# A delta-rule attention and cosine-gated FFN kernel: another order of the same 2196 tasks

## The chip, the cores and the metric

One core of a Trainium2 chip. The time is that of the device for one execution, in microseconds (us); the median of three runs stands for a kernel. Engines are called as in the profile: PE (TensorE; PEld its weight loads), DVE (VectorE), ACT (ScalarE), POOL (GpSimd), SP (SyncE, which here only issues transfers).

## The reference

32 heads (4 batches of 8) run a delta rule over 768 steps with a 48 x 48 state; the outputs, laid side by side, go through a gated FFN.

```python
k_n = k / (np.linalg.norm(k, axis=-1, keepdims=True) + 1e-06)
for t in range(S):                       # S = 768
    y[:, :, t] = q[:, :, t] @ state
    v_old = kt @ state
    state = state + beta_t * outer(kt, vt - v_old)
x = y.transpose(0, 2, 1, 3).reshape(3072, 384)
h = x @ w_in                             # 384 x 2048
g = h * np.cos(h)
out = g @ w_out                          # 2048 x 384
```

## The kernel before, in words

Time is cut into 24 chunks ("units", n = 0 to 23) of 32 steps for all 32 heads. Two units make a pair m; a pair gives 256 tokens, which are one FFN pass p = m (0 to 11).

A unit's tasks are: loads of `k`, `q`, `v` (from unit 8 on `blocks`, a load that feeds a transpose on DVE); `turn` (transposes on PE, copied out by ACT); `gram` (products of keys with keys and queries, 64 matmuls); `gram_keys`, `gram_queries` (DVE); the inverse of a unit triangular matrix; `state` (64 matmuls with the running state); `right` (DVE); `solve` (inverse by right side); `solve_out` (DVE); `update` (32 matmuls) and `update_out` (DVE, the new state); `within` (64 matmuls); `within_out` (ACT); `features` (transposes on PE) and `features_out` (ACT), which give x.

The inverse comes in three ways. Units 0 and 1 are inverted by doubling on PE (`double`, six levels of two halves, 32 matmuls a half here, with copies, transposes and adds between). Pair 1 is inverted in halves, all other pairs whole: the Gram matrix goes to DRAM (`gram_put`), comes back in another layout (`gram_get`), POOL runs `inv` (62 small products and subtractions a pair, 30 for pair 1, lines 818 and 825), and the inverse goes out (`put`) and back (`get`). There is one buffer each for the matrix that comes back, for the inverse and for the tile that `get` fills, so pairs go through this loop one after the other.

FFN passes 0 and 1 run plain: `hidden` (24 matmuls, 2.6 to 2.9 us, a block of h), then `turns`, `rest`, `cos`, `gate` on ACT and DVE, and for pass 0 `out` (8 matmuls of 384 columns, line 1223). From pass 2 on `hidden` is a scheme of 20 `layer` products on sums of blocks (`x_sum`, `in_sums`), and from pass 1 on `out` is seven products per pass on sums of blocks (`left`, `right`), with `collect` on DVE. The sums run on DVE or POOL, by choice.

The weights arrive as 64-bit numbers in 28 transfers (`weights`, t = 0 to 11 of 512 KB for w_in, 12 to 27 of 384 KB for w_out), and each is made into 32-bit ones by `split` (ACT), `shift` (DVE) and `add` (POOL). They land in 8 tiles that also hold the gates.

`warm` tasks (56, line 487) are filler: one product on constants, whose result nobody reads; they are left out once the first `out` product has been emitted, and five more run at the very start.

**What sets the order.** Every task has a number, in the order in which it is added: 0 to 4 the first loads, 5 to 7 beta and the half tiles, 8 to 63 the fillers, 64 `clear`, from 65 the units with the FFN behind them, from 2084 the weights (three numbers in four are split, shift and add). `Order.LINE` lists the numbers in the order in which the tasks are emitted; each engine then runs its own tasks in that order. `Order.OTHER` names the tasks that go to their second choice: a sum to the other of DVE and POOL, a transfer to ACT's queue in place of SP's. Transfers of SP and ACT share eight completion semaphores in turn, so the ninth waits until the first has landed. The cost and due figures given to `add` are not used when the kernel is built.

Of the kernel before, what the change touches and what calls it, by code (L numbers as in the profile page):

```python
# [55 lines left out]
class Order:  # L56

    OTHER = {
        ('gram_put', 2), ('q', 3), ('gram_get', 1), ('inv', 1, 0), ('put', 1), ('gram_put',
        4), ('gram_put', 5), ('v', 7), ('v', 8), ('v', 9), ('blocks', 11, 1), ('gram_put',  # L60
        11), ('put', 5), ('v', 13), ('put', 6), ('gram_put', 15), ('gram_get', 7), ('get',
        15), ('v', 16), ('blocks', 16, 0), ('blocks', 16, 1), ('gram_put', 16), ('blocks',
        18, 1), ('k', 19), ('blocks', 19, 0), ('gram_get', 9), ('get', 19), ('gram_put',
        20), ('v', 21), ('gram_put', 21), ('put', 10), ('gram_put', 22), ('v', 23),
        ('gram_put', 23), ('gram_get', 11), ('right', 4, 4), ('left', 1, 1, 0), ('left', 1,
        3, 0), ('left', 1, 3, 1), ('store', 1, 0), ('x_sum', 2, 'd'), ('x_sum', 2, 'n'),
        ('x_sum', 2, 'm'), ('x_sum', 2, 'e'), ('x_sum', 2, 'k'), ('x_sum', 2, 'g'),
        ('x_sum', 2, 'i'), ('x_sum', 2, 'l'), ('x_sum', 2, 'f'), ('x_sum', 2, 'b0'),
        ('left', 2, 4, 1), ('left', 2, 3, 1), ('x_sum', 3, 'd'), ('x_sum', 3, 'n'),
        ('x_sum', 3, 'm'), ('x_sum', 3, 'e'), ('x_sum', 3, 'k'), ('x_sum', 3, 'g'),  # L70
        ('x_sum', 3, 'i'), ('x_sum', 3, 'l'), ('x_sum', 3, 'h'), ('x_sum', 3, 'b0'),
        ('left', 3, 4, 1), ('left', 3, 3, 1), ('x_sum', 4, 'd'), ('x_sum', 4, 'm'),
        ('x_sum', 4, 'g'), ('x_sum', 4, 'i'), ('left', 4, 3, 0), ('left', 4, 3, 1),
        ('store', 4, 0), ('x_sum', 5, 'd'), ('x_sum', 5, 'e'), ('x_sum', 5, 'l'), ('x_sum',
        5, 'h'), ('x_sum', 5, 'b0'), ('left', 5, 2, 0), ('left', 5, 4, 1), ('left', 5, 3,
        0), ('left', 5, 3, 1), ('store', 5, 0), ('x_sum', 6, 'd'), ('x_sum', 6, 'g'),
        ('x_sum', 6, 'l'), ('x_sum', 6, 'f'), ('x_sum', 6, 'b0'), ('left', 6, 1, 0),
        ('left', 6, 4, 0), ('store', 6, 1), ('x_sum', 7, 'd'), ('x_sum', 7, 'm'), ('x_sum',
        7, 'g'), ('x_sum', 7, 'i'), ('x_sum', 7, 'f'), ('x_sum', 7, 'h'), ('x_sum', 7,
        'b0'), ('left', 7, 4, 0), ('left', 7, 4, 1), ('left', 7, 3, 1), ('x_sum', 8, 'd'),  # L80
        ('x_sum', 8, 'm'), ('x_sum', 8, 'e'), ('x_sum', 8, 'k'), ('x_sum', 8, 'g'),
        ('x_sum', 8, 'l'), ('left', 8, 3, 0), ('store', 8, 0), ('store', 8, 1), ('x_sum', 9,
        'd'), ('x_sum', 9, 'm'), ('x_sum', 9, 'e'), ('x_sum', 9, 'k'), ('x_sum', 9, 'i'),
        ('x_sum', 9, 'l'), ('x_sum', 9, 'b0'), ('left', 9, 1, 0), ('left', 9, 2, 0),
        ('left', 9, 1, 1), ('left', 9, 3, 0), ('store', 9, 0), ('x_sum', 10, 'k'), ('x_sum',
        10, 'i'), ('x_sum', 10, 'l'), ('x_sum', 10, 'h'), ('x_sum', 10, 'b0'), ('left', 10,
        1, 0), ('left', 10, 1, 1), ('left', 10, 4, 1), ('left', 10, 3, 0), ('left', 10, 3,
        1), ('store', 10, 0), ('x_sum', 11, 'd'), ('x_sum', 11, 'e'), ('x_sum', 11, 'k'),
        ('x_sum', 11, 'g'), ('x_sum', 11, 'f'), ('left', 11, 1, 0), ('left', 11, 2, 0),
        ('left', 11, 1, 1), ('left', 11, 3, 0), ('left', 11, 3, 1), ('store', 11, 1),  # L90
        ('store_right', 11), ('weights', 5), ('weights', 7), ('weights', 15), ('weights',
        16), ('weights', 18), ('weights', 20), ('weights', 22), ('weights', 23), ('weights',
        25), ('weights', 27)
# [4 lines left out]
0 1 66 2 70 2084 3 71 4 8 9 72 122 67 68 5 2085 123 69 127 73 128 124 65 75 125 80 76 77 2088 178 78  # L98
82 129 2089 74 2092 64 207 79 81 130 10 2096 132 83 134 181 84 6 179 11 2090 136 135 12 133 87 140
2086 2093 86 210 85 2100 13 14 89 208 90 143 15 88 91 16 2104 141 17 142 182 2097 2094 94 244 211  # L100
183 137 95 2091 185 212 139 138 96 18 93 19 131 144 92 2108 186 215 121 145 2098 245 216 111 184 213
2105 147 97 100 101 20 187 188 2112 98 21 148 2087 22 23 2095 102 268 2101 105 24 146 150 2116 99
2109 189 25 190 217 191 2099 149 103 26 2106 126 269 218 219 106 220 27 104 112 151 2110 107 109 153
221 110 247 251 2107 252 108 152 2113 248 223 2120 28 113 154 249 2124 222 299 114 29 2114 155 2102
156 115 30 2115 117 157 2128 116 2132 160 31 180 2103 2117 118 158 119 120 2136 2125 323 159 168 224
2140 250 272 162 2111 273 163 2121 2133 2118 161 253 2137 169 209 792 225 166 226 254 2122 255 256
227 167 164 32 165 33 170 2119 2138 34 171 172 174 2144 2126 173 274 793 2129 2139 2127 2123 246 228
214 300 35 797 2141 275 276 302 2130 2148 2131 277 175 176 303 2145 2134 794 192 177 2149 193 278
798 306 795 2152 304 307 802 2142 2146 279 194 195 799 2150 196 796 2156 36 197 2135 198 2147 803
804 305 37 199 805 807 270 200 2143 2151 2153 800 201 38 2160 2154 806 203 324 202 308 309 2164 229  # L110
801 812 310 2161 2157 2162 204 205 206 230 808 280 2168 327 813 271 2158 328 231 817 2165 814 232
815 809 233 281 354 378 282 283 234 2166 2169 2159 235 2172 236 2167 816 2176 2155 938 818 7 832 39
40 41 356 931 2163 810 42 237 2173 811 2180 43 2177 2174 822 44 238 357 2184 240 239 284 2170 241
285 827 823 819 2185 2178 935 311 820 833 242 243 45 824 286 2186 821 361 301 2179 825 46 2181 47
258 828 360 48 329 826 49 259 330 860 848 2171 861 829 830 865 2182 831 866 862 870 844 863 867 409
332 287 864 333 871 939 868 2175 936 2183 872 934 2188 869 875 834 334 2187 331 880 873 257 874 260
2192 876 50 382 932 849 358 335 336 2189 2190 325 877 362 433 885 2191 381 261 2193 881 262 2194 878
879 882 264 886 933 263 852 883 890 265 337 887 411 288 266 2195 884 891 289 895 267 338 359 290 888
291 845 856 889 835 892 292 896 355 897 937 383 464 339 947 293 294 836 295 296 838 297 51 298 326
846 313 954 52 415 53 363 379 412 853 488 837 953 941 364 839 365 955 956 893 942 340 964 944 960  # L120
965 384 857 894 466 840 54 416 55 341 901 968 366 957 385 948 898 467 841 387 958 961 966 899 842
342 945 962 946 967 969 959 963 900 903 904 970 850 858 972 417 971 973 56 943 979 388 314 906 854
389 974 413 905 981 386 907 982 909 975 843 976 312 980 315 940 902 436 985 437 911 983 316 847 986
984 390 317 318 949 343 319 912 855 977 320 952 908 987 344 345 913 391 914 438 950 988 989 346 915
991 990 917 57 347 392 470 992 1007 993 321 380 910 322 995 919 348 978 58 994 349 996 414 471 951
393 394 350 920 999 491 1000 1015 997 351 1008 352 395 998 368 353 1016 1066 1009 418 419 1001 420
439 1068 921 1010 1073 440 1067 1011 421 396 1002 922 1003 1069 1005 397 916 442 1004 923 918 1006
1012 443 1017 1074 1013 924 1070 1077 1076 851 1018 1071 1072 367 468 925 1081 1014 1078 1082 1079
1019 1080 927 1075 441 519 859 1085 444 1023 1083 928 1086 1084 369 472 1024 1094 1092 410 929 1095
1093 926 370 59 1020 1036 1021 525 371 434 1098 469 1099 1025 445 1087 1022 1026 398 446 372 374 373  # L130
1035 1038 1096 375 1027 1031 376 1028 399 1029 1097 1032 492 1033 1100 1101 377 1102 1041 400 1030
1034 1104 1088 1103 1039 401 1042 465 1044 1105 1089 1106 402 489 1046 1037 403 1124 1108 404 1125
1090 1091 543 1047 473 405 1040 930 474 1109 447 493 1120 1048 406 1110 475 1049 435 1126 407 423
408 526 1121 1179 1122 448 494 1050 1181 1107 449 1127 495 1051 1052 1111 476 497 1054 1114 496 450
1055 451 1128 452 60 1115 1043 424 1129 1182 1183 1056 1112 1057 1118 1058 1180 498 1130 1123 1045
1119 521 1113 1184 422 522 1186 61 1185 1190 1194 574 1059 1060 1116 1191 1131 598 1132 62 1053 1133
# [1738 lines left out]
```

## Time and profile before

| | us |
|---|---|
| median of three runs (641.67 to 646.46) | 642.42 |
| the profiled execution | 642.72 |
| its span, first to last instruction | 640.9 |
| PE busy, fillers included | 616.0 |
| DVE busy | 510.5 |
| POOL busy | 441.5 |
| ACT busy | 296.4 |
| moved by DMA | 50.38 MB, 79 GB/s mean |

The page gives each engine's busy time and 40 slices of 16 us. The mean granted clock of PE is 0.986. Some landmarks of the timeline, in us from the span's start: solve-0 begins at 47.76, hidden-0-0 at 64.12, solve-2 at 85.81, update-3 at 111.49, and the last matmul ends at 637.2.

### The profile page before, as it was taken

The page shows a single profiled execution, that of the slowest core. Times are in us where ns is not written, and L with a number is a line of the kernel's source. Part 1 is how long each engine was busy: PE and PEld are TensorE (multiplying, and loading weights), DVE is VectorE, ACT ScalarE, POOL GpSimd, SP SyncE. Part 2 cuts the span into 40 slices and gives each one's busy share as a digit, 9 for nine tenths or more (in the row PEclk, how much of TensorE's full clock was granted, in tenths as well). Part 3 has the DMA queues.
Part 4 walks back from the last instruction along what each step waited for, and adds up shares of the span by engine and source line. Part 5 has one row for each costly group of instructions (what it writes and reads, how often), then busy time and mean ns, then how long its engine had stood idle before and what let it go on. Part 6 is the DMA issues. An engine that isn't in the chain of part 4 may idle for free.

```text
span 640.9 us, 25243 instructions
## 1 busy us (share of the span) xinstructions
PE 616.0 (96%) x10688; PEld 570.7 (89%) x10688; DVE 510.5 (80%) x1049; ACT 296.4 (46%) x528; POOL 441.5 (69%) x780
## 2 busy tenths in 40 slices
PE   5877999999999999999999999999999999999997
PEld 4655877897799999999999999999999999999997
DVE  5776877998989899887898888888888786656682
ACT  3444655654334453553642544643643553545440
POOL 5435888888778788788689888886883884112231
PEclk9887999999999999999999999999999999999999
DMA  9777556563551454434536245243304202000000
GB/s 189 200 177 180 113 157 145 93 141 54 100 88 20 98 87 70 86 69 73 88 68 104 49 70 99 49 67 67 74 2 78 45 3 41 19 2 26 2 25 26
DMA packets 209369, 50.38 MB, mean 79 GB/s; under 512 B 200920, under 2 KB 204264, under 8 KB 209256
## 3 DMA queue, kind: packets, MB, share of 16 engines
q1 hardware_dynamic: 161896, 35.03, 28.7%
q10 hardware_dynamic: 47072, 13.25, 10.1%
q8 instruction: 84, 1.38, 0.9%
q0 software_dynamic: 288, 0.50, 0.4%
q14 instruction: 29, 0.24, 0.1%
HBM read 38.51 MB, written 10.22 MB: 76 GB/s over the span
## 4 chain that ended last, share of the span: by engine, by line
PE 82%; DMA 7%; DVE 4%; issue 2%; SPq 2%; POOL 1%; ACT 1%; ACTq 0%; DVEq 0%; POOLq 0%
PE p_out L1281 28%; PE p_h L1199 27%; PE p_h L1025 6%; PE p_out L1223 3%; PE p_kq L869 3%; PE p_s L966 3%; PE p_kq L983 3%; DMA kp<-in_k_dram 3%; PE p_u L941 2%; PE p_g L648 2%; PE p_h L1281 2%; PE p_z L1004 1%; DMA g_ffn<-in_moe_w_in_dram 1%; SPq L392 1%; DMA z_dr<-z 1%
## 5 line engine op out<-in xcount | busy, mean ns | idle before, releaser
L818 POOL TENSOR_TENSOR part<-z,gb 128x126 f32<-128x126 f32 (+23 forms) x321 | 146.1, 455 | 41.8 <-DMA gb<-g_dr 12.9
L825 POOL TENSOR_TENSOR z<-z,part 128x126 f32<-128x126 f32 (+23 forms) x321 | 146.9, 458 | 25.1
L1281 PE MATMUL p_out<-w_out,g_ffn 128*128 128x192 f32 x672 | 121.9, 329 | 0.6 <-DVE o L1333 0.6
L1281 PEld LDWEIGHTS p_out<-w_out,g_ffn 128*128 128x128 f32 x672 | 107.7, 190 | 2.0 <-DVE o L1333 0.9
L1078 ACT ACTIVATE turns<-turns,halfpi 128x512 f32<-128x512 f32 x96 | 68.0, 718 | 55.0 <-DVE turns L1069 43.0
L1281 PE MATMUL p_out<-w_sum,g_ffn 128*128 128x192 f32 x496 | 89.7, 329 | 0.2 <-DVE o L1333 0.2
L1199 PE MATMUL p_h<-x_sum,w_in 128*128 128x128 f32 x640 | 84.0, 277 | 0.0
L1062 ACT ACTIVATE turns<-g_ffn,quarter_turn 128x512 int32<-128x512 f32 x70 | 49.8, 719 | 66.7 <-DVE g_ffn L1216 29.5
L1281 PEld LDWEIGHTS p_out<-w_sum,g_ffn 128*128 128x128 f32 x496 | 79.6, 190 | 1.2 <-issue 0.4
L1199 PEld LDWEIGHTS p_h<-x_sum,w_in 128*128 128x128 f32 x640 | 78.8, 192 | 1.1
L1216 DVE TENSOR_TENSOR g_ffn<-g_ffn,p_h 128x512 f32<-128x512 f32 x80 | 54.2, 680 | 17.3 <-PE p_h L1199 16.4
L1069 DVE SCALAR_TENSOR_TENSOR turns<-g_ffn,turns 128x512 f32<-128x512 f32 x70 | 54.3, 783 | 13.0 <-ACT turns L1062 12.9
L996 ACT COPY y<-p_kq 32x384 f32<-32x384 f32 x96 | 45.1, 470 | 36.4 <-PE p_kq L983 30.0
L1081 DVE TENSOR_TENSOR g_ffn<-turns,g_ffn 128x512 f32<-128x512 f32 x70 | 51.9, 751 | 3.8 <-ACT turns L1078 3.7
L567 POOL TENSOR_TENSOR knrm<-ksum,halves 128x16 f32<-128x16 f32 (+1 forms) x14 | 38.4, 2745 | 22.8 <-DVE ksum L555 20.7
L1199 PE MATMUL p_h<-x_sum,in_sum 128*128 128x128 f32 x400 | 52.9, 277 | 0.0
L1199 PEld LDWEIGHTS p_h<-x_sum,in_sum 128*128 128x128 f32 x400 | 49.7, 192 | 0.8
L1333 DVE SCALAR_TENSOR_TENSOR o<-p_out,o 128x192 f32<-128x192 f32 x74 | 25.1, 351 | 29.3 <-PE p_out L1281 28.8
L1025 PE MATMUL p_h<-x_ffn,w_in 128*128 128x128 f32 x384 | 46.1, 277 | 0.0
L1025 PEld LDWEIGHTS p_h<-x_ffn,w_in 128*128 128x128 f32 x384 | 44.2, 192 | 1.4 <-issue 0.2
L1199 PE MATMUL p_h<-x_ffn,w_in 128*128 128x128 f32 x320 | 42.4, 277 | 0.0
L1297 POOL TENSOR_TENSOR g_ffn<-g_ffn,g_ffn 128x512 f32<-128x512 f32 x18 | 25.4, 1417 | 23.2 <-PE p_out L1281 19.4
(156 smaller groups left out, 1080.8 us busy)
## 6 DMA issues: line engine op xcount, KB each, us to landing
g_ffn<-in_moe_w_in_dram SPq DMA_DIRECT2D x10, 512.0 KB
gb<-g_dr SPq DMA_DIRECT2D x14, 256.0 KB
vp<-in_v_dram SPq DMA_DIRECT2D x68, 48.0 KB
g_ffn<-in_moe_w_out_dram SPq DMA_DIRECT2D x8, 384.0 KB
g_ffn<-in_moe_w_out_dram ACTq DMA_DIRECT2D x8, 384.0 KB
kp<-in_k_dram SPq DMA_DIRECT2D x120, 24.0 KB
out_dram<-o SPq DMA_DIRECT2D x14, 192.0 KB
zt<-z_dr SPq DMA_DIRECT2D x72, 32.0 KB
```

Source lines behind the costliest of these rows:

```text
L567: nc.gpsimd.tensor_tensor(out=scales[m][2][:, part], in0=sums[m, part.start][:, 0:n], in1=halves[:, 0:n], op=ALU.pow,)
L818: eng.tensor_tensor(out=part, in0=z[:, 0:rows, j, None].to_broadcast(shape), in1=a[:, j, None, j + 1 :].to_broadcast(shape), op=ALU.mult,)
L825: eng.tensor_tensor(out=behind, in0=behind, in1=part, op=ALU.subtract)
L996: nc.scalar.copy(by_parity(y[quarter(b)]), p_kq[quarter(b ^ 1), :, b % 2])
L1025: nc.tensor.matmul(p_h[:, i], w_in[:, t, (4 * k + i) * 128 : (4 * k + i + 1) * 128], xts[p][:, t, unit * 128 : (unit + 1) * 128], start=(i ...
L1062: nc.scalar.activation(turns[p, f], hidden_of(p, f), AF.Identity, bias=quarter_turn, scale=TURN)
L1069: nc.vector.scalar_tensor_tensor(out=r, in0=hidden_of(p, f), scalar=TURN, in1=t, op0=ALU.mult, op1=ALU.subtract,)
L1078: nc.scalar.activation(r, r, AF.Sin, bias=halfpi, scale=2.0 * math.pi)
L1081: nc.vector.tensor_tensor(out=place(p, f), in0=step_of(rests.pop((p, f)), f), in1=step_of(hidden_of(p, f), f), op=ALU.mult,)
L1199: nc.tensor.matmul(p_h[:, e], in_block(*w)[:, e], x_of(p, b), start=new and e == 0, stop=True, skip_group_check=True,)
L1216: nc.vector.tensor_tensor(out=part_of(p, to), in0=part_of(p, one), in1=part_of(p, two), op=op)
L1281: nc.tensor.matmul(p_o, left(p, part, a)[:, e % 4], right(e, b), start=(e == 0), stop=(e == FT // 2 - 1), skip_group_check=True,)
```

## The change

Two constants of `Order` are replaced; no task, tile, instruction or size is changed. `WARM_FIRST` (5) and `WARMS` (56) stay, and with the new place of the first `out` two fillers less are emitted (29 for 31). The diff, cut to the beginning of both constants:

```diff
     OTHER = {
-        ('gram_put', 2), ('q', 3), ('gram_get', 1), ('inv', 1, 0), ('put', 1), ('gram_put',
-        4), ('gram_put', 5), ('v', 7), ('v', 8), ('v', 9), ('blocks', 11, 1), ('gram_put',
...
+        ('k', 2), ('gram_put', 2), ('q', 3), ('gram_put', 3), ('inv', 1, 1), ('put', 1),
+        ('q', 5), ('gram_put', 6), ('v', 7), ('gram_get', 3), ('gram_put', 8), ('blocks',
...
     LINE = """
-0 1 66 2 70 2084 3 71 4 8 9 72 122 67 68 5 2085 123 69 127 73 128 124 65 75 125 80 76 77 2088 178 78
...
+8 0 1 9 2084 70 178 66 2088 2 3 71 207 122 181 4 67 10 5 11 68 2092 123 72 179 69 73 127 75 12 128
...
```

Read as names, PE's tasks up to update-3 (a number after "warm" counts fillers in a row; `double` has unit, level and half):

```
before
turn-0 warm2 gram-0 turn-1 double-0-0-1 double-0-0-0 gram-1 warm1 double-0-1-0 double-1-0-0
warm2 double-0-1-1 double-1-1-0 warm3 double-0-2-0 warm2 double-0-2-1 double-1-0-1 turn-2 warm2
double-1-1-1 turn-3 double-0-3-0 double-0-3-1 warm1 gram-2 warm1 double-1-2-0 warm2 double-0-4-1
warm2 gram-3 double-0-4-0 warm2 double-1-2-1 double-0-5-0 double-0-5-1 turn-4 warm1 solve-0
double-1-3-0 warm1 update-0 warm1 within-0 double-1-3-1 double-1-4-0 warm1 features-0 state-1
turn-5 double-1-4-1 gram-4 hidden-0-0 double-1-5-1 double-1-5-0 warm2 solve-1 warm1 update-1
within-1 gram-5 warm1 hidden-0-2 features-1 state-2 turn-6 hidden-0-4 solve_half-2 warm1 between-2
warm1 solve-2 hidden-0-6 update-2 warm1 within-2 gram-6 hidden-0-8 features-2 state-3 turn-7
hidden-0-10 solve_half-3 between-3 solve-3 out-0-0-0 hidden-0-12 update-3

after
warm2 turn-0 warm2 gram-0 turn-1 warm2 gram-1 double-0-0-0 double-0-0-1 warm2 double-0-1-1
double-1-0-1 turn-2 double-0-1-0 warm1 double-0-2-1 warm1 turn-3 warm1 double-0-2-0 gram-2
double-1-0-0 warm2 double-0-3-0 warm1 double-1-1-1 warm2 double-1-1-0 warm1 double-0-3-1 gram-3
warm1 double-0-4-1 double-0-4-0 double-1-2-0 double-0-5-0 turn-4 warm1 double-0-5-1 double-1-3-0
warm1 double-1-2-1 solve-0 warm1 update-0 double-1-4-0 within-0 warm2 features-0 state-1 turn-5
double-1-3-1 hidden-0-0 gram-4 double-1-4-1 double-1-5-0 double-1-5-1 warm2 solve-1 hidden-0-2
update-1 within-1 gram-5 warm1 state-2 features-1 warm1 turn-6 hidden-0-4 warm1 solve_half-2
between-2 solve-2 warm1 update-2 within-2 gram-6 out-0-0-0 features-2 state-3 turn-7 hidden-0-6
solve_half-3 hidden-0-8 between-3 hidden-0-10 solve-3 hidden-0-12 update-3
```

Fillers apart, the two hold the same tasks up to update-3. The transfers of the head, a star for those on ACT's queue (a `k`, `q` or `v` is four transfers, 192 KB together; a `gram_put` 128 KB here):

```
before
weights-0 v-0 weights-1 k-2 weights-2 k-3 weights-3 q-2 weights-4 q-3* weights-5* k-4 weights-6 v-1
q-4 weights-7* k-5 weights-8 gram_put-2* q-5 gram_put-3 weights-9 weights-10 gram_get-1* k-6
weights-11 weights-12 v-2 weights-13 k-7 weights-14 v-3 gram_put-4* weights-15* v-4 put-1*

after
weights-0 k-2* weights-1* k-3 weights-2 q-2 weights-3 q-3* weights-4* weights-5 v-0 weights-6 k-4
k-5 weights-7 v-1 gram_put-2* weights-8 q-4 weights-9* weights-10 k-6 gram_put-3* weights-11*
gram_get-1 q-5* weights-12* k-7 v-2 q-6 weights-13* weights-14* v-3 weights-15 weights-16*
gram_put-4 q-7 put-1*
```

On ACT's own line `k-2` now stands ahead of the first `square-0-0`, and `weights-1` ahead of `turn_out-0`. POOL's adds of the weights and `inv-1` are shuffled (`inv-1-0` moves from DVE to POOL, `inv-1-1` the other way), and `beta_home` comes early on DVE. Later in the kernel the same kinds of tasks are permuted: 51 `x_sum` and 32 `left` sums change between DVE and POOL (`left` on POOL: 33 before, 29 after; `x_sum` 46 and 47), two `right` sums and one of `in_sums` likewise, and 74 groups of transfers change queue.

## The prediction

> **What bounds the kernel now.** I read the page's engine totals and slices first, then who TensorE (PE) waited for, the chain of waits, PE's timeline over the first 100 us and the windows table.
>
> ```profile
> span 640.9 us, 25243 instructions
> PE 616.0 (96%) x10688; PEld 570.7 (89%) x10688; DVE 510.5 (80%) x1049; ACT 296.4 (46%) x528; POOL 441.5 (69%) x780
> PE   5877999999999999999999999999999999999997
> DMA  9777556563551454434536245243304202000000
> q8 instruction: 84, 1.38, 0.9%
> ```
>
> PE is full from the fifth slice on; only the head has room. "Busy" includes the filler products of line 487 (72 matmuls, whose rows in the timeline sum to 26 us), all before 92.6 us. Idle (640.9 - 616.0 = 24.9 us) plus filler is 51 us, the most that any order could save. The last line is PE's code: 84 packets for 2 x 10688 instructions, 254 each, so one packet for every 127 matmuls with their weight loads.
>
> ```profile
> PE p_u L935 <- issue: 4.0, 2, 2.7
> PE p_g L648 <- issue: 3.3, 3, 1.7
> PE p_out L487 <- issue: 1.6, 1, 1.6
> ```
>
> These waits end on nothing that the profile names. In PE's timeline they stand in the middle of one product:
>
> ```profile
> 16.47 0.42 PE L648 MATMUL p_g<-kq_t 48*32 48x64 f32 x4 [1.18 <-issue]
> 29.45 0.81 PE L487 MATMUL p_out<-o 128*128 128x256 f32 x3 [1.59 <-issue]
> 35.12 0.83 PE L648 MATMUL p_g<-kq_t 48*32 48x64 f32 x47 [1.66 <-issue]
> 44.73 0.73 PE L710 MATMUL p_h<-in_sum 32*32 32x32 f32 x62 [0.93 <-issue]
> 51.24 0.31 PE L935 MATMUL p_u<-vp,in_sum 32*32 32x48 f32 x10 [2.70 <-issue]
> 87.96 0.28 PE L935 MATMUL p_u<-g_ffn,w_sum 32*32 32x48 f32 x4 [1.28 <-issue]
> ```
>
> Counted from the start they stand at matmul 218, 471, 597, 852, 977 and 1992: whole multiples of some 126.7 apart. They are ends of code packets. The trace's DMA records give each packet's start, and for each I subtract the time at which PE crossed the boundary before: 1.04, 4.63, 3.10, 2.44, 1.17, 3.95, 1.89, 1.67, 1.82, 2.25 us for the ten from 17.51 to 66.80 (mean 2.4), and 0.4 to 1.9 for most later ones. The packet then takes 0.9 to 1.5 us, and PE goes on 1.35 to 1.5 us after it. So a boundary costs nothing if PE needs over about 3.5 us (1.04 + 1.08 + 1.39) to work through a packet, and up to 7 where transfers are outstanding: at 44.73 two weight loads had just been issued (43.93, 44.55) and the packet started 3.95 us later. The six waits sum to 9.3 us.
>
> ```profile
> 48.54 2.70 issue
> 52.80 1.56 PE p_s L966 x32
> 54.36 1.15 PE p_out L487 x2
> 69.38 4.59 DMA z_dr<-z
> 86.68 1.28 issue
> ```
>
> The chain of waits holds only two of them, 2.70 and 1.28. Before 40 us it runs over the loads of k, q and the weights, later over the inverse and its trip through DRAM.
>
> ```profile
> 50.00:60.00 10.00, 8.34 (x240) 6.09 (x243) 7.62 (x20) 2.41 (x6) 4.43 (x4) 0.66 0.68 178
> ```
>
> In this window the granted clock is 0.66, after the 2.70 us wait. update-0, filler and within-0 take 4.2 us there (chain, 52.80 to 56.99); the same three from 91.11 take 2.26. So the slow clock costs 1.9.
>
> The Trainium skill (TensorE: Matmul & The Clock Gate, Part 1) puts a halved clock after an idle window of some 3.4 us; here 2.70 us of idle was followed by it.
>
> **The change, part by part.** All 2196 tasks stay. I lay the new PE order out by matmuls per task (64 for a gram or state, 32 for an update or half a doubling level, 24 for a hidden, 2 for a filler). On the old order this puts matmul 218 at the 61st of gram-1 and 977 in solve-0, as the trace has it.
>
> *Start.* Loads k-2 and weights-1 go to ScalarE's queue, ahead of square-0-0 and turn_out-0. In their lane places the old order's v-0 was issued from 8.01 to 10.74 and weights-1 until 11.24; ScalarE can only go on after that. So square-0-0 moves from 8.43 to about 10.8 and turn_out-0 from 8.84 to 11.3; behind them wait sum-0-0, the roots on POOL and gram-0: the first doubling starts 2.4 us late. Against that q-2 and q-3 have a weight and a load less ahead (704 KB, 3.7 us at the 192 GB/s of the first 50 us). q-4, which turn-4 needs, moves behind weights-7, k-5, gram_put-2 and weights-8 (4928 KB ahead become 6272): 7.0 us. Its last part was issued at 34.66; with 4.5 us to land (the chain's kp loads: 4.0 to 5.8) it is there at 46.2, where turn-4 ran at 45.53. Solve-0 is still behind turn-4, so the early gains end there. Value: 0.
>
> *Solve-0.* Its boundary stays in it (25th of 64 instead of the 55th), and the one before is in turn-4. Between them PE has half a turn, two fillers, three half levels (0.45 to 0.65) and 24 matmuls: about 3.4 us. At the mean queue time a packet needs 2.4 + 1.1 + 1.4 = 4.9, leaving a wait of 1.5 for 2.70; at the ends 0.1 and 3.7. But turn-4 comes 0.7 later. Gain 0.3 (-1.0 to 2.6). Half of the slow clock goes with a wait of that size (35.12's 1.66 left 0.83 in its window): 1.0 (0 to 1.9).
>
> *Solve-2.* Its boundary moves from the 61st matmul to its end. A wait there lies beside solve_out (1.02 on DVE), which update-2 needs anyway: gain 1.2 (0 to 1.28).
>
> *Filler.* Six instead of seven after hidden-0-0, where PE has other work: 0.65 (0 to 0.7).
>
> *Blocks without FFN work.* hidden-0-0 moves ahead of gram-4, hidden-0-2 behind solve-1, and hidden-0-6 behind state-3, out-0-0-0 (2.75 us) ahead of it. Between matmuls 1358 and 1485 PE now has two and a half half levels, two fillers and 38 matmuls of solve-1, 2.8 us; before, hidden-0-0 (3 us) lay in it. The packet needed 2.25 + 0.93 + 1.4 = 4.6 there. It stands before solve_out-1, behind which DVE has update_out-1 and a weight's shift. Loss 1.8 at most, none if the copies and adds between the levels fill it: 1.0. Likewise 1612 to 1738 (2.4 us of matmuls, hidden-0-2 gone) and 1992 to 2118 (3.1 us, hidden-0-6 gone), where packets needed 3.6 and 3.8: 0.5 each (0 to 1.9 together), as DVE's update_out (0.94) and solve_out run meanwhile.
>
> *After 115 us.* PE then idles 1.3 us in all. The left sums on POOL fall from 33 to 29 (1.27 us each, 0.69 to 0.74 on DVE): DVE has 4 to 18 us idle in each 50. The inverse loop has little room: put(3) 172.17, put(4) 210.43, put(5) 252.28; z is back about 4 us after the gets' last issue (176.76, 216.69, 259.16), and solve-6, 8 and 10 start at 181.5, 223.43 and 264.58: slack 0.7, 2.7, 1.4. By PE work ahead, solve-6 comes 2.1 later and 8 and 10 come 2.4 earlier. Loss 0.8 (0 to 3).
>
> Sum: 0.3 + 1.0 + 1.2 + 0.65 - 1.0 - 1.0 - 0.8 = 0.35. The profiled execution took 642.72 (span 640.9), 0.3 over the median of 642.42: 642.4, or 642.1 as a median.
>
> **Rivals.**
> *Packets come early (0.20).* If queue times fall to 1.0, the head gives 2.6 + 1.9 + 1.28 + 0.65, and the earlier q-2 and q-3 net 1.3 (3.7 less 2.4): 7.7, or 634.7. For: eight of the first ten packets came within 1.9 us of being needed. Against: the bytes are the same, and weights issued by solve-1 rise from 10880 to 11840 KB with the loads.
>
> *Packets come late (0.16).* The new order has four packets without FFN work from 1358 to 2118, the old one two (which cost 0.49 and 1.28). If they queue like the one at 44.73, each needs 3.95 + 1.05 + 1.35 = 6.4 against some 3.0 of work; three of four so hit cost 3 x 3.4 - 1.8 = 8.4: 650.8. It decides from a queue time of about 3.3. For: the earlier weights just named. Against: old queue times from 64 to 94 us were 0.7 to 2.3.
>
> *The inverse loop binds (0.12).* A head that gains, with POOL's loop not earlier, gives it back at solve-8 and solve-10: 2.4 + 1.0 in place of the 0.8 above, 642.1 + 2.6 = 644.7.
>
> *Crossing a packet costs nothing (0.05).* Were the gaps something else that stays, only order noise is left: 642.4.
>
> The Trainium skill (Runtime: NRT & Kernel Launch, Instruction fetch mechanics) says that crossing a 16 KiB block is mostly hidden, and gives PE room for 2048 instructions; by that this last rival would hold. The trace agrees on 16 KB but not on hidden: six gaps, 9.3 us.
>
> **How the numbers follow.** The forecast, losses and gains near balance, has 0.47. A measurement here tells about 1% (6.4 us) from no change. Faster: the first rival and a tail of the forecast, 0.20 + 0.02. Slower: the second, with tails of the third and the forecast, 0.16 + 0.03 + 0.04. Same: 0.55. The range runs between the first two rivals' times, 634.5 to 650.5, which leaves a part of each outside.
>
> **What would show it.** square-0-0 at 10.8 and gram-0 near 12.4; turn-4 at 46 or later; a gap inside solve-0 after its 24th matmul, about 1.5 us; granted clock above 0.66 in 50 to 60; a gap inside solve-1 where there was none; no gap inside solve-2; idle ahead of solve-8 or solve-10. I am wrong if turn-4 runs well before 45 (the loads are faster than by bytes), if update-3 ends over 3 us from 112.3, or if PE idles over 4 us after 120.

## The result, and the profile after

The new order is slower by about 1%: 649.94 us (median of 12 runs, 646.39 to 653.01) against 643.18 (639.08 to 646.46), ratio 1.0105 [1.0082, 1.0128]. That is 6.8 us, inside the forecast's range and on the other side of its forecast of 642.1.

The page of the new order (profiled execution 649.79, span 648.0): engine totals, PE's busy tenths, the granted clock and DMA in 40 slices, and the code packets.

```profile
span 648.0 us, 25196 instructions
PE 618.8 (95%) x10684; PEld 571.4 (88%) x10684; DVE 511.2 (79%) x1051; ACT 295.5 (46%) x528; POOL 433.6 (67%) x778
PE   6688879999999999999999999999999999999997
PEclk8989899999999999999999999999999999999999
q8 instruction: 84, 1.38, 0.9%
```

The span grew by 7.1: PE is busy 2.8 longer with two fillers (four matmuls) less, and idle 4.3 longer. Both are to be explained. Some of PE's waits, in us in total, times and longest:

```profile
PE p_g L648 <- issue: 4.6, 2, 3.4
PE p_out L1281 <- DVE o L1333: 1.6, 2, 1.2
PE p_kq L869 <- issue: 1.6, 1, 1.6
PE p_u L941 <- DMA zt<-z_dr: 1.0, 1, 1.0
PE p_u L935 <- issue: 0.9, 1, 0.9
```

The 2.70 in solve-0 and the 1.28 in solve-2 are gone. New are a code wait of 0.9 in solve-1, one in state-2 (L869) and, far behind the head, waits for DVE (L1333) and for z (L941). ("Code wait" is used for a wait at the end of a code packet.) PE's timeline shows where they stand:

```profile
32.23 0.33 PE L648 MATMUL p_g<-kq_t 48*32 48x64 f32 x11 [3.41 <-issue]
46.18 0.63 PE L615 MATMUL p_t<-consts,qp 128*128 128x128 f32 x4 [1.98 <-DMA kp<-in_k_dram]
67.80 0.52 PE L935 MATMUL p_u<-rhs,w_sum 32*32 32x48 f32 x26 [0.94 <-issue]
77.36 0.81 PE L869 MATMUL p_kq<-st,kq_t 48*64 48x48 f32 x21 [1.61 <-issue]
87.61 0.88 PE L935 MATMUL p_u<-g_ffn,w_sum 32*32 32x48 f32 x64 [0.84 <-DVE g_ffn L919]
93.43 0.54 PE L648 MATMUL p_g<-kq_t 48*32 48x64 f32 x35 [1.24 <-issue]
326.36 0.68 PE L941 MATMUL p_u<-rhs,zt 64*64 64x48 f32 x30 [0.96 <-DMA zt<-z_dr]
400.14 1.57 PE L1281 MATMUL p_out<-w_out,g_ffn 128*128 128x192 f32 x8 [1.23 <-DVE o L1333]
```

67.80, 77.36 and 93.43 are matmuls 1485, 1740 and 2119 from the start: the ends of the three packets that the prediction named as having no FFN work. The 3.41 in gram-2 (32.23) lies ahead of solve-1, to which the new order still comes earlier.

Landmarks tell where the time went. Up to solve-1, up to solve-2 and up to update-3 the two orders have done the same tasks, fillers apart.

| us from the start | before | after | after less before |
|---|---|---|---|
| solve-1 | 69.06 | 66.24 | -2.8 |
| solve-2 | 85.81 | 87.61 | +1.8 |
| update-3 | 111.49 | 114.54 | +3.05 |
| last matmul ends | 637.22 | 644.33 | +7.1 |

So the new order leads by 2.8 at solve-1, loses 4.6 on the 20 us to solve-2, 1.25 more to update-3, and 4.06 in the long rest ("the tail" from here on). Of the 4.6, 4.5 are lost by the start of solve_half-2 (82.64 before, 84.35 after); the way from there to solve-2 takes 3.26 for 3.17. The chain of waits of after, between solve-1 and solve-2, whole lines in order of time, with the places marked where lines are left out:

```profile
66.86 0.94 issue
67.80 0.52 PE p_u L935 x26
68.32 2.88 PE p_h L1025 x24
...
75.31 1.11 SPq L841
...
79.30 1.63 DMA w_sum<-z_dr
80.94 0.34 DVE w_out L529
...
81.74 1.09 DVE w_out L529
82.83 1.29 DVE g_ffn L524
84.12 1.09 DVE w_out L529
...
87.09 0.47 DVE g_ffn L919
87.57 0.04 issue
87.61 0.93 PE p_u L935 x64
```

Behind the code wait in solve-1 the chain runs over the way back of pair 1's inverse (`get` on SP, L841, until 80.94) and then through DVE: three steps of the weights' `shift` (L524, L529) and steps of a norm stand ahead of between_out-2 (L919), for which solve-2 waits. The 1.61 in state-2 is not on this chain, so by the profile its removal alone would not have brought solve-2 forward in this execution; in e6 and e10 below, which have the same order here, the chain does run through state-2's wait (1.08 and 0.52) and then over ACT and the same DVE steps. Before, two fillers stood between solve_half-2 and solve-2, and solve-2's one wait was the 1.28 of code.

### The profile page after: what moved, and what is told of

Its sections match the earlier page's. It is cut to its first block, busy times and chain, and to the rows that moved or that the text cites. A ratio compares the mean times of both kernels' runs of the same rounds, so it can differ in the third digit from the quotient of the medians.

```text
span 648.0 us, 25196 instructions
## 1 busy us (share of the span) xinstructions
PE 618.8 (95%) x10684; PEld 571.4 (88%) x10684; DVE 511.2 (79%) x1051; ACT 295.5 (46%) x528; POOL 433.6 (67%) x778
## 4 chain that ended last, share of the span: by engine, by line
PE 73%; DMA 7%; DVE 6%; POOL 5%; SPq 3%; issue 2%; ACT 2%; ACTq 1%; DVEq 0%; POOLq 0%
PE p_out L1281 24%; PE p_h L1199 23%; PE p_h L1025 6%; PE p_out L1223 4%; PE p_kq L869 3%; PE p_s L966 3%; POOL part L818 2%; DMA kp<-in_k_dram 2%; POOL z L825 2%; PE p_kq L983 2%; PE p_g L648 2%; PE p_u L941 2%; DMA g_ffn<-in_moe_w_in_dram 2%; SPq L392 1%; PE p_z L1004 1%
## 5 line engine op out<-in xcount | busy, mean ns | idle before, releaser
L818 POOL TENSOR_TENSOR part<-z,gb 128x126 f32<-128x126 f32 (+24 forms) x321 | 144.5, 450 | 39.8 <-DMA gb<-g_dr 15.9
L825 POOL TENSOR_TENSOR z<-z,part 128x126 f32<-128x126 f32 (+24 forms) x321 | 143.8, 448 | 25.2
L1281 PE MATMUL p_out<-w_out,g_ffn 128*128 128x192 f32 x672 | 124.0, 330 | 1.9 <-DVE o L1333 1.6
L1281 PE MATMUL p_out<-w_sum,g_ffn 128*128 128x192 f32 x496 | 88.2, 328 | 0.0
L1297 POOL TENSOR_TENSOR g_ffn<-g_ffn,g_ffn 128x512 f32<-128x512 f32 x14 | 18.8, 1346 | 66.7 <-PE p_out L1281 45.4
L1069 DVE SCALAR_TENSOR_TENSOR turns<-g_ffn,turns 128x512 f32<-128x512 f32 x70 | 53.0, 759 | 8.5 <-ACT turns L1062 8.3
L1333 DVE SCALAR_TENSOR_TENSOR o<-p_out,o 128x192 f32<-128x192 f32 x74 | 25.0, 350 | 30.3 <-PE p_out L1281 26.9
L1025 PE MATMUL p_h<-x_ffn,w_in 128*128 128x128 f32 x384 | 45.8, 277 | 0.0
L1211 ACT COPY p_h<-p_h 128x512 f32<-128x512 f32 x40 | 22.9, 573 | 46.0 <-PE p_h L1199 33.1
```

Source lines behind the costliest of these rows:

```text
L818: eng.tensor_tensor(out=part, in0=z[:, 0:rows, j, None].to_broadcast(shape), in1=a[:, j, None, j + 1 :].to_broadcast(shape), op=ALU.mult,)
L825: eng.tensor_tensor(out=behind, in0=behind, in1=part, op=ALU.subtract)
L1025: nc.tensor.matmul(p_h[:, i], w_in[:, t, (4 * k + i) * 128 : (4 * k + i + 1) * 128], xts[p][:, t, unit * 128 : (unit + 1) * 128], start=(i ...
L1069: nc.vector.scalar_tensor_tensor(out=r, in0=hidden_of(p, f), scalar=TURN, in1=t, op0=ALU.mult, op1=ALU.subtract,)
L1281: nc.tensor.matmul(p_o, left(p, part, a)[:, e % 4], right(e, b), start=(e == 0), stop=(e == FT // 2 - 1), skip_group_check=True,)
```

## The experiments

Each kernel ran side by side with the kernel before; ratios are to that. Orders are given as names, PE's tasks unless an engine is named.

**Head or tail.** Three splices of the two orders at a task behind which both have done the same work.

```diff
 e1: before's order through update-3
+    then after's order
 e2: after's order through update-3
+    then before's order
 e3: after's order through hidden-0-0
+    then before's order
```

> Every engine's order and every choice of engine or queue is the old one through update-3 and the new one behind it. My theory: the new kernel is 7.1 us longer in the profile because its head loses 3.0 us by update-3 and its steady part 4.1 us behind it; this kernel then pays only the 4.1: ratio to before about 1.006. Rival A, the whole loss is the head's (the later waits follow from it): 1.000. Rival B, the whole loss is the steady part's: 1.011.

> The other way round: new order through update-3, old behind it. My theory: 3.0 us over before, ratio about 1.005, update-3 begins at 114.5 in the profile and the old steady part adds no wait of its own. Rival A (all in the head): 1.011. Rival B (all behind it): 1.000, which needs update-3 to begin near 111.5.

> New order through hidden-0-0, old behind it. In the profiles the new order begins features-0 1.9 us and hidden-0-0 4.05 us earlier, with the gram-4 and doubling work put off. My theory: that lead of some 2 us is real, and what loses it and 5 us more is the new order from solve-1 to out-0-0-0, whose code packets hold no FFN work; with the old order there the lead stays: 2 us under before, ratio 0.997, and no gap in state-2 or gram-6. Rival: the lead is not worth anything, because the weights or the inverse of pair 1 set solve-2 (82.6 to 85.8 in before) whatever comes first: ratio 1.000 to 1.003, solve-2 at 85.8 or later.

Measured: e1 648.83, 1.0092 [1.006, 1.0124]; e2 651.24, 1.0137 [1.0098, 1.0176]; e3 643.47, 1.0009 [0.9983, 1.0035]. The splices bring waits of their own at the seam, 2.0 us in e1 (hidden-1-0) and 4.0 in e2 (hidden-0-14), so the two shares can't be added; by the medians both halves of the new order lose, against both rivals, which put all in one of them. e3 says more: the new order's lead at hidden-0-0 is worth nothing (0.997 was expected), and by the medians of e2 and e3 the head's loss lies behind that point. But e3's profiled execution, the slowest of its twelve (647.59), lost in the old order as well: 48.3 us from solve-1 to update-3 (before: 42.4), with a code wait of 1.56 in solve-1, whose packet has lost hidden-0-0 here too, and one of 2.38 in gram-5, at matmul 1613, where the packet had queued 4.2 us (before: 0.7).

**The two loads on ACT.** after with k-2 and weights-1 back on SP's queue.

```diff
 OTHER = {
-    ('k', 2), ('weights', 1),
```

> The new kernel with loads k-2 and weights-1 on SP's queue instead of ScalarE's, nothing else changed. All theories: square-0-0 back near 8.4 and gram-0 near 10. My theory: turn-4 still waits for q-4 until about 46, so solve-0 begins within 0.5 us of the new kernel's 50.36 and the time stays within 2 us of the new kernel (ratio to before 1.008 to 1.011). Rival: the 2.7 us late start is carried through: solve-0 near 48, ratio 1.006.

Measured: 648.56, 1.0093 [1.0058, 1.0127]. gram-0 came at 9.9 for 12.7 and solve-0 at 48.7 for 50.4, nearer to the rival's 48; but update-3 came no earlier (115.8 for 114.5), and the tail's 529.8 stayed. The late first doubling is real, and the lead of 1.7 at solve-0 that its removal gives is gone by update-3.

**Covering the empty packets.** e5 puts an FFN group into the second packet without one, e8 also into the third.

```diff
 e5, on after:
 gram-5 warm1
+hidden-0-4
 state-2 features-1 warm1 turn-6
-hidden-0-4
 e8, further:
 solve-2 warm1
+hidden-0-6
 update-2 within-2 gram-6 out-0-0-0 features-2 state-3 turn-7
-hidden-0-6
```

> The new order with one group moved: hidden-0-4 runs directly before state-2 instead of behind turn-6, so the code packet during which the new order has no feed-forward group holds one, and its boundary falls on state-2's 19th matmul instead of its 44th. Theory (the 1.61 us wait inside state-2 and the half clock behind it delay right-2, and with it solve_half-2 and solve-2): the wait goes, solve_half-2 starts near 82.4 instead of 84.35, solve-2 near 85.7 instead of 87.61, ratio to the kernel before 1.007 to 1.008 against 1.0105 for the new order. Rival (the inverse and VectorE set solve-2 in any case): solve-2 stays at 87.6, ratio 1.0105 or above, the group's own time being added ahead of it.

> The new order with two groups moved: hidden-0-4 directly before state-2 as in the run above, and hidden-0-6 directly before update-2, behind solve-2, so that the second packet without feed-forward work holds one too. Theory: besides the 1.61 us in state-2, the 1.24 us wait in gram-6 and the half clock at 94.6 to 98.0 go (out-0-0-0 2.7 us instead of 4.38), update-3 starts 3 to 5 us before 114.54, ratio to the kernel before 1.003 to 1.006, the rest being the tail's. Rival (the waits only move with the packet's end to the next task, and the groups lengthen the way to solve-2 or update-2 by their own time): update-3 at 114 to 116, ratio 1.010 or above.

Measured: e5 651.34, 1.012 [1.0074, 1.0165]; e8 649.58, 1.0101 [1.0071, 1.0131]. Neither can be told from the new order's 1.0105, so neither theory held. The code waits in state-2 and (e8) in gram-6 went, and others took their place. PE's timeline of e8:

```profile
81.04 1.19 PE L1019 MATMUL p_w<-rhs,w_sum 32*32 32x48 f32 x64 [1.23 <-ACT kq_t L745]
82.86 0.88 PE L1019 MATMUL p_v<-g_ffn,in_sum 32*32 32x48 f32 x64 [0.62 <-ACT g_ffn L1031]
86.32 1.50 PE L1055 MATMUL p_u<-g_ffn,w_sum 32*32 32x48 f32 x64 [2.58 <-DVE g_ffn L1039]
```

solve_half-2 (81.04) now waits 1.23, and solve-2 (86.32) 2.58 for DVE's between_out-2. One group of 2.9 us covers either the packet or the way from state-2 to solve-2 over ACT and DVE; in the old order hidden-0-2 lay in the packet, and hidden-0-4 covered the way. DVE in the same execution, with the idle time in brackets:

```profile
80.39 1.17 DVE L649 TENSOR_SCALAR w_out<-w_out 128x384 uint32<-128x384 uint32 x1
81.47 1.37 DVE L644 SCALAR_TENSOR_TENSOR g_ffn<-g_ffn 128x384 uint32<-128x384 uint32 x1
82.77 1.17 DVE L649 TENSOR_SCALAR w_out<-w_out 128x384 uint32<-128x384 uint32 x1
84.06 0.99 DVE L700 TENSOR_TENSOR krec<-knrm 128x16 f32<-128x16 f32 x1
85.72 0.55 DVE L1039 TENSOR_TENSOR g_ffn<-rhs,p_v 128x384 f32<-128x384 f32 x1
```

between_out-2 (85.72) stands behind two shifts and a norm.

**Moving the packets instead of the work.** before, with fillers left out so that each packet ends 12 matmuls later in the work. (Five fillers of two matmuls at the start and one behind turn-0; the expectation names the places wrongly.)

```diff
-    WARM_FIRST, WARMS = 5, 56
+    WARM_FIRST, WARMS = 0, 56
 turn-0
-warm2
+warm1
 gram-0
```

> The kernel before, its order untouched, with 12 filler matmuls fewer on TensorE (5 at the start, 7 behind turn_out-0), so that every code packet's end falls 12 matmuls later in the work: the one inside solve-0 and the one inside solve-2 come to lie outside the solves, the next in the same stretch in the gram of layer 1. Theory (the 2.70 us in solve-0 and the 1.28 us in solve-2 are late code, fixed to the matmul's number): both waits vanish from the solves, the solve's end and update-0 come 1.5 to 2.7 us earlier, the wait reappears outside the solves or not at all, ratio 0.995 (0.992 to 0.999). Rival (the waits belong to the products' data, or the fillers kept the clock up and their lack costs 1 to 2 us): the waits stay at the same matmuls of the solves, ratio 1.000 to 1.003.

Measured: 644.23, 1.0019 [0.9995, 1.0043]. PE's timeline:

```profile
46.37 0.89 PE L1053 MATMUL p_u<-vp,in_sum 32*32 32x48 f32 x63 [0.73 <-ACT kq_t L743]
50.76 0.45 PE L828 MATMUL p_h<-w_sum 32*32 32x32 f32 x31 [3.46 <-issue]
75.76 1.01 PE L766 MATMUL p_g<-kq_t 48*32 48x64 f32 x50 [2.93 <-issue]
```

The wait left solve-0 (46.37, 63 of its 64 matmuls in one piece) and stands behind it at the same matmul number, 977 (50.76). So these waits are code, bound to the count of matmuls and not to the data. The time did not fall: a wait just behind the solve costs as much, and the packet that ends at matmul 1613 cost 2.93 inside gram-5. Before, it ended at gram-5's third matmul, just behind a wait for the new state (0.49), and cost nothing. The place is not the reason, since e3 lost 2.38 at before's place: the packet queued 4.6 us here, 4.2 in e3 and 0.7 before.

**The tail's two waits.**

```diff
 e6, on after:
 SP:
+get-13
 k-20
-get-13
 DVE:
-right-16
 collect(5,5)
+right-16
```

> The new order with two steps put back ahead of what the search placed before them: get-13 ahead of k-20's transfers on SyncE's queue, right-16 behind the last step of collect(5,5) on VectorE. Theory (the tail's loss is new waits on other engines that the search made by moving small steps): TensorE's 0.96 us at solve-13 and 1.23 us at out-5-5-0 go, the time from update-3 to the last matmul falls from 529.8 to about 527.6, ratio to the kernel before 1.007. Rival (the waits move to the next task, the tail is bound elsewhere): the two gaps shrink but the stretch stays at 529 to 530, ratio 1.0105.

Measured: 648.27, 1.0076 [1.005, 1.0103]; update-3 to the last matmul 528.4, between theory and rival. The wait at solve-13 is gone, so it was get-13's place: in after SP issued it at 322.06, behind k-20's eight transfers from 316.87. The other wait moved one product ahead, and ACT's timeline of e6 shows why:

```profile
396.53 0.72 ACT L1198 ACTIVATE turns<-turns,halfpi 128x512 f32<-128x512 f32 x1 [7.95 <-DMA g_dr<-g]
397.16 0.58 ACT L1331 COPY p_h<-p_h 128x512 f32<-128x512 f32 x1
```

ACT did nothing for 7.95 us, because transfers of its own queue (block loads, a Gram store) were waiting in its line; cos(6) and the copy that PE needed came behind them.

**All repairs at once, and the queues by themselves.** e9 is e8 with between_out-2 ahead of shift-16, get-13 as in e6, and five transfers back on SP. e10 is after with all such transfers of the tail on SP; e12 is before with 38 more of them on ACT.

```diff
 e9, on e8:
 OTHER = {
-    ('blocks', 20, 1), ('blocks', 21, 0), ('v', 19), ('gram_put', 18), ('put', 8),
 DVE: right-2 shift-17
+scale-3-0
 shift-15
+between_out-2
 shift-16
-scale-3-0 between_out-2
 e10, on after:
 OTHER = {
-    ('v', 7), ('gram_get', 3), ('k', 12), ('k', 13), ('gram_put', 8), ('blocks', 10, 1),
...
 SP:
+get-13
 k-20
-get-13
 e12, on before:
 OTHER = {
+    blocks and gram_put of the tail
```

> The new order with all repairs that the traces suggest. Head: the two feed-forward groups moved as in the run before (hidden-0-4 ahead of state-2, hidden-0-6 ahead of update-2), and on VectorE between_out-2 ahead of the weights' shift-16, which took it 2.2 us too late there. Tail: get-13 ahead of k-20 on SyncE, and blocks-20-1, blocks-21-0, v-19, gram_put-18 and put-8 back from ScalarE's queue to SyncE's, since ScalarE stood 6.79 us on such transfers with cos(6) behind them. Theory (feed-forward groups cover either a packet or the way over VectorE to solve-2, and the tail waits on a queue that stands in ScalarE's line): solve_half-2 to solve-2 shrinks from 5.3 us to about 3.3, VectorE's 2.58 us wait ahead of solve-2 to under 0.8; the waits at solve-13 and out-5-5-0 go without a new one, update-3 to the last matmul 527.5 instead of 529.8; ratio to the kernel before 1.003 to 1.005. Rival (another chain stands right behind each): solve-2 waits as long on something else, the stretch stays above 528.4, ratio 1.008 or above.

> The new order, its head untouched; behind update-3 the 37 transfers that go to ScalarE's queue (all but the stores of passes 9 to 11) are put on SyncE's, and get-13 stands ahead of k-20. Theory (the tail's waits of 2 us, which came back at another place in each repaired version, come from transfers standing in ScalarE's own line: ScalarE stood 6.79 us ahead of cos(6) and 7.16 us ahead of collect(3,1) on them): no wait above 0.5 us behind update-3, update-3 to the last matmul 526.8 to 527.3 (the 525.7 of the old order and five more changes of kind at 0.2), ratio to the kernel before 1.005 to 1.007. Rival (SyncE's queue becomes the late one, or the waits come from the order of the products themselves): waits of 2 us or more in all stay or grow, stretch at or above 528.4, ratio 1.008 or above.

> The kernel before, its order untouched; behind update-3 the 38 block loads and Gram stores that go to SyncE's queue are put on ScalarE's, which then has 78 transfers there for 40. Theory (transfers in ScalarE's line hold up the activations and copies behind them, and TensorE has too little slack to cover it): TensorE's waits behind update-3 grow from 0.9 us to 3 us or more, ratio to the kernel before 1.004 or above. Rival (ScalarE is busy less than half of the time and absorbs them): waits under 1.5 us, ratio 0.998 to 1.002.

Measured: e9 648.12, 1.0094 [1.0063, 1.0124]; e10 655.1, 1.0165 [1.012, 1.0209]; e12 670.83, 1.0425 [1.0392, 1.0459]. In e9 solve_half-2 to solve-2 shrank to 3.4 and DVE's wait to 0.68, as expected, but a code wait of 1.42 followed behind solve-2; the tail's two waits went, and one of 1.97 came at features-11, behind another ACT line that stood 7.16 us on a store. The time is the rival's, about that of the new order: the repairs removed most of the waits that they were made for (0.92 stayed in gram-6), and other waits stood elsewhere. That the repairs brought the one at features-11 is not shown, since e5, with the tail unrepaired, has it too (1.92, behind an ACT line that stood 7.07). e10's theory did not hold either: solve-12 waited 2.75 for z, whose inverse's `put`, now on SP as well, was issued at 309.65 for 302.17 in after. e12 bears out the cost of ACT's line: PE's waits in the tail grew from 0.9 to 18.5 us. Its longest, in PE's timeline, and the clock behind it, by the windows (length, then busy us and instructions of PE, PEld, DVE, ACT and POOL, granted clock, DMA share, GB/s):

```profile
220.64 0.90 PE L1160 MATMUL p_z<-consts,y 128*128 128x128 f32 x3 [4.17 <-ACT y L1152]
```

```profile
220.60:224.00 3.40, 3.36 (x113) 2.94 (x116) 0.29 (x1) 1.67 (x3) 3.01 (x8) 0.50 0.20 33
```

**The price of changing the kind of product.** before, with 21 FFN tasks put between two attention tasks that stood side by side, for example:

```diff
-update-6 within-6 out-1-2-0
+update-6 out-1-2-0 within-6
```

> The kernel before with 21 more changes from attention products to feed-forward products after update-3: at 21 places two attention tasks that stood side by side get one feed-forward task between them, nothing else moves. In the traces the first matmul of a feed-forward task behind an attention task takes 0.307 us where one behind another feed-forward task takes 0.109. Theory (that 0.2 us is a real cost of each change, and the new order's five or six more changes are 1.0 to 1.2 us of its tail): update-3 to the last matmul grows by 21 x 0.198 = 4.2, from 525.7 to 529.9, ratio to the kernel before 1.0065. Rival (the longer record is only how the end of a pipelined matmul is drawn, and costs nothing): 525.5 to 526.5, ratio 0.999 to 1.002.

Measured: 650.74, 1.0107 [1.0065, 1.0148]; update-3 to the last matmul 535.9 for 525.7. The first matmuls of 0.307 us (0.36 for `out`) rose from 63 to 85, and PE's busy time in the tail by 5.3; 22 x 0.198 is 4.4 of that. So the rival, by which the longer record costs nothing, is out; the theory's 4.2 is only part, as PE's waits rose by 5.1 as well, on ACT's copies above all, whose sources came later.

## Why the prediction was wrong

The experiments left several executions of the same order up to update-3: before, e1, e11 and e12 of the old one, after, e2, e6 and e10 of the new. (e4, the new order but for two loads' queue, fits in: 48.5.) From solve-1 to update-3:

| | old, four executions | new, four executions |
|---|---|---|
| solve-1 begins | 67.4 to 70.3, mean 68.5 | 64.9 to 67.2, mean 66.3 |
| solve-1 to update-3 | 41.6 to 42.4, mean 42.0 | 46.1 to 49.6, mean 48.1 |
| PE's waits over 0.2 in it | 3.0 to 3.8, mean 3.4 | 6.1 to 6.7, mean 6.4 |
| of them code waits | 0.7 to 1.3, mean 1.1 | 3.3 to 4.1, mean 3.8 |
| PE busy in it | 38.4 to 38.5 | 40.0 to 43.1, mean 41.6 |
| granted clock | 1.00 in all | 0.90 to 0.96 |

One line of the windows for each order, of e1 and of after:

```profile
67.40:109.10 41.70, 38.37 (x1081) 33.51 (x1080) 33.77 (x67) 24.66 (x49) 34.07 (x53) 1.00 0.61 140
```

```profile
66.24:114.54 48.30, 41.62 (x1078) 35.33 (x1078) 34.48 (x65) 24.32 (x48) 36.42 (x64) 0.93 0.56 125
```

**The step that failed: "Blocks without FFN work", 2.0.** It named the three packets rightly (1358, 1612 and 1992) and undersized them. In after their waits were 0.94, 1.61 and 1.24 for 1.0, 0.5 and 0.5, by the mean of the four executions 1.0, 1.0 and 1.5. Through the first packet PE took 2.9 us (63.94 to 66.86), the bare matmuls, and then waited. The other two needed 4.9 and 4.6 us from one end to the next where the forecast had 3.6 and 3.8, taken from the old order: they queued 2.56 and 2.04 for 1.25 and 1.18. In the other three executions of each order it was 1.6 to 3.6 for 0.6 to 1.2. Why they queue longer in the new order is not shown. Less what the old order lost in solve-2, code waits grew by 2.8. All other waits in the stretch stayed nearly the same, 2.6 for 2.3: the new order waits bare ahead of between-2 and solve-2 (0.65 and 0.84 in after), the old one ahead of between-3 and solve-3 (0.65 and 0.73).

The larger part had no term in the step: the half clock behind the waits. PE is busy 3.1 longer with the same products and one filler less, and the more so the lower the granted clock: 40.0 at 0.96 (e2), 41.6 at 0.93 (after, e10), 43.1 at 0.90 (e6). I had priced the half clock as a gain behind solve-0 and nowhere as a loss; out-0-0-0 alone took 4.38 for 2.68, from its start to the next task's, under it. Code waits and half clock are 5.9 of the 6.1 that the stretch grew by; the forecast had 2.0, less the 1.2 of solve-2.

This is an account by the profile's rows; no change to the head gave the time back, since in e5, e8 and e9 other waits took the place of those removed. And it is no property of the new order alone: with late packets the old one lost as much in the profiled executions of e3 and e7 (48.3 and 48.5 from solve-1 to update-3, at a clock of 0.93).

**"After 115 us", 0.8, was the second.** solve-6, 8 and 10 did not wait; the loop did not bind where I put it. Yet the tail lost 4.06, and executions with an unspoiled tail agree on it: update-3 to the last matmul is 525.2 to 526.1 with the old tail (before, e3, e7) and 529.0 to 529.8 with the new (after, e4, e5, e8). 2.0 of it are waits, which e6 and e9 trace to small steps standing behind transfers in the lines of SP and ACT, at places where I had looked at POOL's loop only. 1.0 is five more changes from attention to FFN products at 0.2 (68 for 63), whose price e11 shows. The last 1.0 lies in longer records of single matmuls, most of them the first behind a wait; this is argued from their list and was not tried by itself.

**The steps that held.** gram-0 came at 12.68 for 12.4; solve-2's wait left it; the gains up to solve-1 came out as 2.3 by the means of the table, against 0.3 + 1.0 (the filler's 0.65 lies behind solve-1). "Value: 0" of the start held in time (e4), but not for its reason: turn-4's second half ran at 46.18 for the 46.2 of the forecast, and yet in e6, with the same loads, it ran at 44.05 without a wait, so in that execution the load was there. In after the wait stands at matmul 850, an end of a packet, and the packet needed there landed at 44.49: code or load, the rows leave it open. Of the three signs that I had set for being wrong two came: turn-4 began at 43.57, well before 45, and update-3 ended at 115.44, 3.1 from 112.3 and so just over the 3 allowed; PE idled 3.3 behind 120. The last two were wide, as each lets a loss of about half of the measured one through.

**One execution was taken for the kernel.** The 2.70 in solve-0 was 0.41, 0.11 and 2.15 in the other three executions of that order, with queue times of 3.95, 1.16, 1.20 and 3.48. My gain from it rested on the largest.

**The rivals.** "Packets come late" gives the time (650.8 for 649.9) by the right places, but not by its condition: the three packets queued 1.37, 2.56 and 2.04, below its 3.3. It, too, had no half clock and no tail, so the agreement of the times is luck. "Packets come early" had something for it up to solve-1: the new order's first ten queue times are 1.7 by the mean, for 2.4. "The inverse loop binds" is out, as solve-8 and solve-10 did not wait, and "crossing costs nothing" is out by e7.

The Trainium skill (Runtime: NRT & Kernel Launch, Instruction fetch mechanics) has the crossing of a block mostly hidden. In the head it is not, and e7 shows it best, as the wait stays at matmul 977 when the work moves past it; in the tail it is, with one code wait of 0.49 in before and none over 0.2 in e7.

Whether packets queue longer behind the weights' loads is only hinted at. Over the 14 profiles, 16 packets of the head in each (matmul 345 to 2246), those whose turn came within 1 us behind the issue of a weights load queued 2.1 us on average (53 of them), the others 1.5 (171). And the same packet of the same order queued from 0.9 to 5.3 us in different executions (the third, new order), a spread wider than that difference.

No kernel here is faster than the one before; e3 and e7 can't be told from it. Open is whether the tail's 2 us of waits can be removed at all in this order: after the repairs of e6 and e9 another of 1.32 and of 1.97 was there.

## What to carry to other kernels

A long product may cover more than one thing, here a code packet or the way over ACT and DVE to the next solve: when it is moved, price the way that it leaves bare, not only the one that it covers at its new place. Where TensorE's waits follow each other, price the half clock behind them as well as the waits. And read a wait of variable size from several executions before its removal is counted as a gain, and a searched order's small moves (a transfer in an engine's line, a change of kind) by their number times their price.

## What the runs showed of the hardware

- **The clock.** Single waits of 0.96 and 1.23 (after, tail), 1.32 (e6) and 1.97 (e9) left the granted clock at 1.00; those of 2.2 to 4.2 in e12 were followed by 0.50 to 0.61 for 3.4 us or more. In the head, where shorter waits follow each other, 1.61 was enough (after, 0.50 from 77.5 to 80.9), and a wait of 1.24 at the same matmul was followed by 0.51 in after and by 1.00 in e2, so the length of a wait alone does not decide. The Trainium skill (TensorE: Matmul & The Clock Gate, Part 1) gives an idle window of some 3.4 us; here less idle did it.
- **DVE beside POOL.** `shift`'s TENSOR_SCALAR on 128x384 takes 0.34 to 0.36 us alone and 1.17 while POOL adds weights; a 128x16 product took 1.01 in place of 0.17. DVE and POOL in after, in the same moments:

```profile
81.66 1.17 DVE L529 TENSOR_SCALAR w_out<-w_out 128x384 uint32<-128x384 uint32 x1
85.33 1.01 DVE L580 TENSOR_TENSOR krec<-knrm 128x16 f32<-128x16 f32 x1
81.35 3.64 POOL L533 TENSOR_TENSOR w_out<-w_out,g_ffn 128x384 uint32<-128x384 uint32 x3 [3.44 <-DVE w_out L529]
85.29 1.01 POOL L533 TENSOR_TENSOR w_out<-w_out,g_ffn 128x384 uint32<-128x384 uint32 x1 [0.30 <-DVE knrm L578]
```

 The Trainium skill (SBUF — State Buffer, Who interferes with whom) says that the two engines hold a shared pair of ports by an exclusive lock; the durations agree, being about one add of POOL (1.0 to 1.2) and not a share of it.
- **Change of kind.** The first FFN matmul behind `within`, `solve`, `gram`, `state` or `update` takes 0.307 us for 0.109 (in `out` 0.36 for 0.16); behind `features`, whose products are 128x128 as well, it is not longer in 11 of 12 places of after. The other way round the first attention matmul takes 0.16 to 0.22, whichever kind stands before it.
